# Sliding-window attention: computing the 64-query edge halves of the score blocks in sets of their own

## Chip, cores, metric

One Trainium2 chip, one core of it. The metric is the device time of one execution in microseconds (us), median of several. A profile is one execution; its span is some 2 us shorter than the time (339.9 against 341.89 us before). A quoted median is that of all executions. A ratio of two kernels is the mean time of the one's fast runs over that of the other's of the same rounds on the same chip, so it is not quite the ratio of the medians quoted beside it.

## What is computed

A transformer block on 2048 tokens of 640 features, bf16: adaptive layer norm, attention with 32 heads of 20 features in a causal window of 256 keys, residual, adaptive layer norm, gated MLP of width 1536, residual.

```python
mod = (_silu(c) @ w_mod).reshape(c.shape[0], 6, 1, -1)   # sa, ca, ga, sb, cb, gb
h = _layernorm(x, axis=-1) * (1 + ca) + sa
# attention: H = 32, Dh = 20, W = 256
mask = (idx[:, None] - idx[None, :] >= 0) & (idx[:, None] - idx[None, :] < W)
p = _softmax(jnp.where(mask[None, None], scores, -1000000000.0), axis=-1)
x = x + ga * attention(h)
h = _layernorm(x, axis=-1) * (1 + cb) + sb
x = x + gb * ((_sigmoid(h @ w_gate) * (h @ w_up)) @ w_down)
```

## The kernel before

A recording layer collects all operations with what they read and write. A list scheduler with a cost model, steered by tuned priorities (the table TIMES), then gives each engine its fixed order; at run time each engine takes its instructions in that order and waits on semaphores. Loads and stores all go through one issuing engine, in order as well.

The tokens are worked in six chunks of 2, 2, 4, 4, 2, 2 blocks of 128. For one group of four heads (they lie in four row groups of TensorE) a score set fills up to 512 columns for each head of one PSUM tile of four banks:

```python
def sc(e, eng, st=st, Sp=Sp):                     # scores, keys on partitions
    for (g, kb, q0, n) in st:                     # n blocks of 128 queries against key block kb
        for j in range(4):
            ins = mm(e, Sp.ap[:, j, off:off + n * 128],
                     kt.ap[32 * j:32 * j + DH, gl, (kb % 4) * 128:(kb % 4) * 128 + 128],
                     qt.ap[32 * j:32 * j + DH, gl, (q0 % 4) * 128:(q0 % 4 + n) * 128],
                     True, True, tp=(32 * j, 0))
        off += n * 128
# ... exponential S -> E on ScalarE (ACT), mask in place on GpSimd, then O += V'E on TensorE
p_S = Pool("S", [nc.alloc_psum_tensor("S0", [128, 4, 512], F32)])           # one buffer
p_E = Pool("E", [sb(f"E{i}", [128, 4, 512])[:] for i in range(4)] + ...)     # and weights not yet or no more in use
p_x1 = sbpool("x1", 8, [128, D]);  p_stg = sbpool("stg", 6, [128, 512]);  p_V = sbpool("V", 10, ...)
```

A key block of 128 meets three query blocks; in the first and in the last of them half of the products are masked away.

The softmax here doesn't subtract the row's maximum and nothing guards it: scores larger than these inputs give would overflow.

## Time and profile before

| | before |
|---|---|
| time | 343.07 us (341.72 to 344.42) |
| span of the profile | 339.9 us |
| TensorE busy / idle | 330.0 / 9.9 us |
| mean granted TensorE clock | 0.999 |
| TensorE matmuls | 3813 |

"Busy" counts the time in which an engine executes; it says nothing of how fast. The granted clock says that: in the records it is 1.0 or 0.5. The lines of this profile are shown in the prediction. In all views PE is TensorE, PEld its weight loads, DVE VectorE, ACT ScalarE, POOL GpSimd and SP the engine that issues the transfers.

### The profile page before, as it was taken

What the parts mean: (1) busy time and instruction counts of PE and PEld (TensorE: products, weight loads), DVE (VectorE), ACT (ScalarE), POOL (GpSimd) and SP (SyncE); (2) the same over time, 40 slices, a digit from 0 to 9 for tenths busy, and PEclk for the clock granted to TensorE, in tenths of its full rate; (3) what the DMA queues carried; (4) which work ended last, traced back from release to release, by engine and by line L of the source; (5) the groups of instructions that cost most, each with busy time, mean ns of one, the idle gap of its engine ahead of it and who ended that gap; (6) DMA issues with size and microseconds to landing.
All of it is one profiled execution on the core that took longest, in us unless ns stands there. A gap on an engine that the chain in (4) does not pass through costs nothing.

```text
span 339.9 us, 9584 instructions
## 1 busy us (share of the span) xinstructions
PE 330.0 (97%) x3813; PEld 201.2 (59%) x3813; DVE 227.6 (67%) x493; ACT 226.9 (67%) x229; POOL 178.4 (52%) x301
## 2 busy tenths in 40 slices
PE   7799989999999999998999999999999999999996
PEld 2577646655555656564765433466545446788884
DVE  4576599999776889646977446398746874554432
ACT  1377878888888888896887798956678851022230
POOL 5132564797666999555675566656656850010000
PEclk9999999999999999999999999999999999999999
DMA  6966689889987752472064101302740122112101
GB/s 211 353 202 181 191 235 257 288 270 209 231 282 253 224 194 41 151 226 60 2 180 115 48 31 65 111 3 40 162 123 12 49 22 72 44 35 41 39 3 39
DMA packets 50990, 44.99 MB, mean 132 GB/s; under 512 B 16513, under 2 KB 46850, under 8 KB 50946
## 3 DMA queue, kind: packets, MB, share of 16 engines
q1 hardware_dynamic: 50946, 44.38, 45.4%
q8 instruction: 30, 0.49, 0.6%
q14 instruction: 14, 0.11, 0.1%
HBM read 28.90 MB, written 12.19 MB: 121 GB/s over the span
## 4 chain that ended last, share of the span: by engine, by line
PE 92%; DMA 4%; SPq 1%; DVE 1%; ACT 1%; issue 0%; ACTq 0%; DVEq 0%
PE M L842 74%; PE S L843 8%; PE O L843 7%; PE M L843 3%; DMA big<-in_w_mod_dram 2%; DMA oT<-doc 1%; SPq L764 1%; DMA doc<-On 1%; ACT hT L984 0%; DVE x L937 0%; DVE V L1020 0%; DVE hT L1005 0%; ACT stg L1019 0%; DVE x L1316 0%; DVE big L1306 0%
## 5 line engine op out<-in xcount | busy, mean ns | idle before, releaser
L1188 ACT ACTIVATE E<-S 128x2048 bf16<-128x2048 f32 (+1 forms) x64 | 118.0, 1844 | 20.9 <-PE S L843 19.6
L842 PE MATMUL M<-h2T,wgu 128*128 128x256 bf16 (+1 forms) x720 | 114.6, 309 | 0.0
L842 PEld LDWEIGHTS M<-h2T,wgu 128*128 128x128 bf16 x720 | 67.2, 98 | 36.6 <-issue 5.5
L1199 POOL TENSOR_SCALAR_AFFINE_SELECT E<-E 128x512 bf16<-128x512 bf16 x89 | 59.9, 683 | 23.3 <-ACT E L1188 21.6
L1201 POOL TENSOR_SCALAR_AFFINE_SELECT E<-E 128x512 bf16<-128x512 bf16 x78 | 50.4, 655 | 31.8 <-ACT E L1188 27.5
L1306 DVE SCALAR_TENSOR_TENSOR big<-sig,M 128x256 bf16<-128x256 f32 (+1 forms) x72 | 36.4, 506 | 41.7 <-PE M L842 20.2
L1304 ACT ACTIVATE sig<-M 128x256 f32<-128x256 f32 (+1 forms) x72 | 32.4, 452 | 44.1 <-PE M L842 43.5
L842 PE MATMUL M<-wd,big 128*128 128x320 bf16 x384 | 56.5, 299 | 0.0
L842 PEld LDWEIGHTS M<-wd,big 128*128 128x128 bf16 x384 | 36.5, 98 | 16.0 <-issue 1.7
L843 PE MATMUL S<-QT,KT 20*128 20x256 bf16 (+2 forms) x832 | 36.2, 258 | 0.0
L926 DVE BATCH_NORM_STATS2 st<-x 128x6 f32<-128x320 bf16 x64 | 27.3, 477 | 7.2 <-DMA x<-in_A_x_dram 7.1
L1249 DVE STREAM_TRANSPOSE T<-O 128x512 f32<-128x512 f32 x32 | 22.6, 708 | 12.6 <-PE O L843 12.5
L843 PEld LDWEIGHTS S<-QT,KT 20*128 20x128 bf16 x832 | 12.3, 92 | 26.5 <-ACT E L1188 9.4
L1316 DVE TENSOR_TENSOR x<-M,x 128x320 bf16<-128x320 f32 x32 | 15.5, 484 | 18.3 <-PE M L842 17.8
L842 PE MATMUL M<-wv,hT 128*128 128x320 bf16 x160 | 27.4, 300 | 0.0
L842 PE MATMUL M<-wo,oT 128*128 128x320 bf16 x160 | 25.8, 300 | 1.5 <-DMA oT<-doc 1.4
L932 POOL TENSOR_SCALAR st<-st 128x2 f32<-128x2 f32 (+1 forms) x11 | 3.0, 274 | 40.4 <-DVE st L929 40.4
L842 PE MATMUL M<-hT,wk 128*128 128x512 bf16 (+1 forms) x100 | 23.1, 354 | 1.1 <-DVE V L1020 1.0
L1258 DVE STREAM_TRANSPOSE On<-Tn 128x512 bf16<-128x512 bf16 x32 | 22.5, 704 | 0.5
L842 PE MATMUL M<-hT,wq 128*128 128x512 bf16 (+1 forms) x100 | 22.7, 356 | 0.0
L843 PE MATMUL O<-E,V 128*32 128x256 bf16 (+2 forms) x568 | 21.1, 262 | 0.0
L1019 ACT ACTIVATE stg<-M 128x512 bf16<-128x512 f32 (+1 forms) x31 | 16.5, 534 | 6.6 <-PE M L842 6.2
(85 smaller groups left out, 386.3 us busy)
## 6 DMA issues: line engine op xcount, KB each, us to landing
x<-in_A_x_dram SPq DMA_DIRECT2D x32, 160.0 KB, 4.1
big<-in_w_mod_dram SPq DMA_DIRECT2D x15, 320.0 KB, 5.5
doc<-On SPq DMA_DIRECT2D x16, 256.0 KB, 2.2
KT<-dk SPq DMA_DIRECT2D x6, 512.0 KB, 5.1
QT<-dq SPq DMA_DIRECT2D x6, 512.0 KB, 4.7
out_dram<-x SPq DMA_DIRECT2D x16, 160.0 KB, 1.8
wgu<-in_B_w_gate_dram SPq DMA_DIRECT2D x5, 384.0 KB, 4.1
dq<-stg SPq DMA_DIRECT2D x15, 128.0 KB, 3.2
```

What stands on the lines that cost most here:

```text
L842: return e.matmul(o, l, r, start=st, stop=sp, skip_group_check=True)
L843: return e.matmul(o, l, r, start=st, stop=sp, tile_position=tp, skip_group_check=True)
L926: ins = e.bn_stats(v(bi * 12 + j * 6, 6), src[bi].ap[:, j * 320:(j + 1) * 320])
L1019: return e.activation(dst(), src(), ACT.Copy)
L1188: A("act", lambda e, eng, E=E, Sp=Sp, ncol=ncol: e.activation(E.ap[:, :, 0:ncol], Sp.ap[:, :, 0:ncol], ACT.Exp, scale=SM_SCALE), c_act(4 * ...
L1199: return e.affine_select(ap, ap, pattern=[[0, 4], [1, 128]], compare_op=ALU.is_ge, fill=0.0, base=0, channel_multiplier=-1)
L1201: return e.affine_select(ap, ap, pattern=[[0, 4], [-1, 128]], compare_op=ALU.is_ge, fill=0.0, base=-1, channel_multiplier=1)
L1249: A("dve", lambda e, g: e.transpose(T1.ap[:], O.ap[:]), 0.71, reads=[O.r()], writes=[T1.r()], prio=4, tag="tr1")
L1258: A("dve", lambda e, g: e.transpose(On.ap[:, half * 512:half * 512 + 512], Tn.ap[:]), 0.71, reads=[Tn.r()], writes=[On.r(half)], prio=7, t ...
L1304: A("act", lambda e, g, pg=pg, sg=sg: e.activation(sg.ap[:, 0:W], pg.ap[:, 0:W], ACT.Tanh, scale=0.5), c_act(W), reads=[pg.r()], writes=[s ...
L1306: A("dve", lambda e, g, pu=pu, sg=sg, ft=ft: e.scalar_tensor_tensor(out=hv(ft), in0=sg.ap[:, 0:W], scalar=1.0, in1=pu.ap[:, 0:W], op0=ALU. ...
L1316: A("dve", lambda e, g, ps=ps, bi=bi, half=half: e.tensor_tensor(x1[bi].ap[:, half * 320:half * 320 + 320], ps.ap[:, 0:320], x1[bi].ap[:, ...
```

## The change

The intent: a key block's first and last 64 queries have only half of their keys valid. The change computes these halves with tiles of 64 keys by 64 queries, two of them (from two key blocks) on one set of columns: partitions 0 to 63 from the one, 64 to 127 from the other. Eight pairs make a set C of 512 columns with an exponential of its own. The main pieces get a set each, and the masks write the edges from C beside them into an E tile of 768 columns. 92 score sets become 76, 60 main ones and 16 of edges.

```diff
-PVLAG = 2
-PVG = [3, 3, 2, 3, 3, 3]
+PVLAG = 1
+PVG = [2, 2, 1, 2, 2, 2]
-    p_x1 = sbpool("x1", 8, [128, D])
+    p_x1 = sbpool("x1", 6, [128, D])
-    p_stg = sbpool("stg", 6, [128, 512])
+    p_stg = sbpool("stg", 5, [128, 512])
-    p_V = sbpool("V", 10, [128, H * VW + 10])
-    p_E = Pool("E", [sb(f"E{i}", [128, 4, 512])[:] for i in range(4)] + ...
+    p_V = sbpool("V", 9, [128, H * VW + 10])
+    p_E = Pool("E", [sb(f"E{i}", [128, 4, 768])[:] for i in range(3)] + ...
+    p_C = sbpool("C", 1, [128, 4, 512])
...
+    def mmc(e, o, l, r, st, sp):                       # a full-array matmul as four of 32 columns of weights
+        for j in range(0, 128, 32):
+            ins = mm(e, o[j:j + 32], l[:, j:j + 32], r, st, sp, tp=(0, j))
...                                                     # early transposes of x:
-                            ins = mm(e, ps.ap[:, bi * 128:(bi + 1) * 128], ...
+                            ins = mmc(e, ps.ap[:, bi * 128:(bi + 1) * 128], ...
...
+                for (g, kb, hf, u, n, off) in items:    # hf: half of the key block, None for a main piece
+                    p0, kn = 64 * (hf or 0), 128 if hf is None else 64
+                    for j in range(4):
+                        ins = mm(e, Sp.ap[p0:p0 + kn, j, off:off + n * 64],
+                                 kt.ap[32 * j:32 * j + DH, gl, k0:k0 + kn],
+                                 qt.ap[32 * j:32 * j + DH, gl, q0:q0 + n * 64], True, True, tp=(32 * j, p0))
...
+                for (rule, c_, u) in spreads:           # edges: mask reads C, writes E
+                    mask(C, cu + c_, 1, E, u, rule, [C.r()])
...
-    (gate broadcast by 20 matmuls of 320 columns)
+    (gate as a column by 50 matmuls of 64 columns, transposed, written to memory and read back to all partitions)
-TIMES = { ... }
+TIMES = { ... }                                        # a new order for every engine
```

PVLAG and PVG say by how many sets the products with V follow the scores. Not shown here: the tables of priorities, the modulation sums in the S tile at the start, finer loads of the first weights, the last output in two halves. The early transposes are split because a split one keeps TensorE in the tiling of the projections around it (in the profile before a change of tiling costs about 0.11 us, worked out in the prediction).

## The prediction

What it reckons with, as the profile before shows it: full-array matmuls of 64, 256, 320 and 512 columns start 29, 109, 136 and 216 ns apart, thus 0.42 ns a column (2.4 GHz) and 2 to 3 ns a matmul. Its "cold matmuls" are those up to 4.7 us, where 512 columns take 0.43 us from start to start in place of 0.216. On GpSimd a memset of 64 columns takes 156 ns and one of 512 columns 525 ns.

> **What bounds the kernel now.** I read the page first: busy times, then the chain that ended last.
>
> ```profile
> span 339.9 us, 9584 instructions
> PE 330.0 (97%) x3813; PEld 201.2 (59%) x3813; DVE 227.6 (67%) x493; ACT 226.9 (67%) x229; POOL 178.4 (52%) x301
> ...
> PE 92%; DMA 4%; SPq 1%; DVE 1%; ACT 1%; issue 0%; ACTq 0%; DVEq 0%
> ```
>
> TensorE is on the chain for 92% of the span. Busy is not full speed, so I took the timeline of TensorE apart, from the start of one group of matmuls to the start of the next:
>
> ```profile
> 258.29 0.40 PE L843 MATMUL S<-QT,KT 20*128 20x128 bf16 x16
> 258.62 0.40 PE L843 MATMUL O<-E,V 128*32 128x256 bf16 x8
> ...
> 259.40 1.53 PE L842 MATMUL M<-wo,oT 128*128 128x320 bf16 x10
> 260.86 0.40 PE L843 MATMUL S<-QT,KT 20*128 20x256 bf16 x8
> ```
>
> A score set S streams 512 columns through four row tiles at once: 512 / 2.4 GHz = 0.213 us. It takes 0.33 us until the next group starts, so the change of tiling costs 0.117 us. The ten full-array matmuls should take 10 x (320 / 2.4 GHz + 3 ns) = 1.36 us and take 1.46: again 0.10. I use 0.11 us for each change of tiling. Over the whole instruction order, TensorE has 293.5 us of columns, 237 changes of tiling (26 us) and some 5 us of the 3 ns; the rest up to 339.9 is the start (first projection at 13.2 us, some 7 us of it lost), about 3 us of later idle gaps, the end (about 3 us) and cold matmuls.
>
> There is a second clock, the loop of the score sets. The next view is the timeline of TensorE and of ScalarE (ACT) in one stretch.
>
> ```profile
> 137.38 0.40 PE L843 MATMUL S<-QT,KT 20*128 20x384 bf16 x8
> ...
> 139.78 0.40 PE L843 MATMUL S<-QT,KT 20*128 20x256 bf16 x8
> ```
>
> ```profile
> 137.83 1.88 ACT L1188 ACTIVATE E<-S 128x2048 bf16<-128x2048 f32 x1 [0.52 <-PE S L843]
> 140.23 1.88 ACT L1188 ACTIVATE E<-S 128x2048 bf16<-128x2048 f32 x1 [0.52 <-PE S L843]
> ```
>
> There is one S tile of four PSUM banks, so a set must be read by its exponential before the next set is written: 0.40 (scores to their last end) + 0.05 + 1.88 + 0.07 = 2.40 us from start to start. That is the shortest spacing of two full sets. The kernel before runs at a median of 2.61 us, with other matmuls between, so this loop hardly costs TensorE anything today.
>
> [...] the trace has 40 of the 64-column modulation matmuls in 1.18 us, 29.5 ns each. [...] No run here shows yet how 64x64 score edges pack, which have eight tiles but only four row groups. [...]
>
> **The change part by part.** Each key block's first and last 64 queries have only half of the keys valid. The change computes these halves apart, with 64x64 tiles, eight edges to one set of 512 columns, and lets the mask write them into a 768-column E tile.
>
> 1. Score columns. Before, 84 sets of 512 and 8 of 384 columns = 46,080, or 19.2 us. After, 76 sets of 512 = 38,912, or 16.2 us. Saved 3.0 us. The gate's broadcast by 20 matmuls of 320 columns (2.7 us) becomes 50 of 64 columns (1.3 us) and a trip through memory. Saved in all **4.3 us**: the total of all columns goes from 293.5 to 289.1. PV keeps its 46,080 columns.
> 2. Changes of tiling. I counted them in the instruction order: 237 before, 211 after. 26 x 0.11 = **2.9 us** saved.
> 3. Start. The modulation sums move out of the M pool and are ordered so that only ten matmuls, not forty, follow the last landing (10.40 us, then 1.2 us of them). About **1 us** saved. The last output in two halves: **0.3 us**.
> 4. Small matmuls. TensorE gets 1114 more. 16 edge sets of 64 matmuls take 0.21 us if eight tiles run together, 0.43 if four[...]. I take **1.5 us** lost in all.
> 5. ScalarE. 92 exponentials become 76 and a few split ones: about 169 to 143 us. Off the path by itself; TensorE is the bound.
> 6. GpSimd. 240 masks of 512 elements before and after. At 0.68 us each (the L1199 group) a set's four masks take 2.7 us, which is as long as the loop, but 178 us of 340 leaves room, unless runs of 64 elements are slower.
>
> So far 4.3 + 2.9 + 1.3 - 1.5 = 7 us, a faster kernel by 2%.
>
> 7. The loop comes back. With less TensorE work between score sets, the instruction order after has places where two sets follow each other with less than 2.40 us of work between their starts. With the durations above, six early gaps and one that is a C set followed at once by a main set (2.07 us short) sum to 5.5 us short; the gaps in the last two-block chunk are 1.7, 1.1, 1.1, 1.9, 1.1 and 1.7 us, short by 5.7 us. TensorE takes its instructions in order, so it must wait: **11.2 us**, against 1.3 us by the same count before. Net **9.9 us** lost.
>
> Why is nothing else put there? The larger E tiles are paid for with SBUF: the pool x1 goes from 8 to 6 buffers. The output projection of the fourth chunk (four blocks) then gets its last two blocks only when the third chunk's down projection has released them. Before, it ended at 228.3 us and its normalisation ran beside that down projection:
>
> ```profile
> 228.29 0.49 DVE L1277 TENSOR_TENSOR x<-M,x 128x320 bf16<-128x320 f32 x1
> 228.70 1.66 DVE L926 BATCH_NORM_STATS2 st<-x 128x6 f32<-128x320 bf16 x4
> ...
> 242.41 1.69 DVE L948 TENSOR_SCALAR h2T<-h2T,scB,shB 128x512 bf16<-128x512 bf16 x5
> ```
>
> From the last residual add to the modulation are 14 us, which TensorE spent on other work. In the new order only 9.5 us of TensorE work lie between that last output projection and the chunk's first gate matmul. So some 5 us of waiting there follow from a second count too. These two counts describe the same idle time and are not added.
>
> Sum: 339.9 - 7.0 + 9.9 = 342.8 us of span. Some 3 us of idle before (waits for transfers) may fall into the same gaps, so I take 341. The profiled run was 2 us longer than its span (341.89 against 339.9); with the median at 343.07 and the fast run at 341.7, I write 342.5.
>
> **The rivals.** (a) TensorE's sum decides and the loop doesn't bite: 333 us of span, some 335 us. For it: 97% busy, and exponentials in the new kernel are fewer. Against it: the order is fixed, and the 2.40 us are measured. (b) The masks become the bound: with 64-element runs at 1 us a mask, four masks take 4 us a set, PV comes late and E buffers (five or six in place of seven, three in place of four in the third chunk) hold up exponentials: 350 us or more. The trace can't tell, since no such mask is in it; 683 ns for 512 elements is far from a fixed cost, so I expect no great change. (c) The gain is hidden behind transfers. The view of stretches (busy of PE, PEld, DVE, ACT, POOL; the last three columns are clock, DMA share, GB/s) has DMA 85% busy up to 100 us:
>
> ```profile
> 20.00:100.00 80.00, 78.83 (x1103) 48.51 (x1092) 64.71 (x144) 65.92 (x75) 48.91 (x75) 1.00 0.85 234
> 160.00:280.00 120.00, 119.98 (x1365) 63.26 (x1364) 82.61 (x173) 93.12 (x74) 76.30 (x120) 1.00 0.26 68
> ```
>
> The first gate matmul, at 106.2 us, can't run before its weights are there. Savings before it then vanish as idle time: 340 us of span. This pulls in the same direction as my step 7.
>
> **Range and chances.** Range 336 to 349: its low end is step 7 at a third of its size, its high end rival (b) in part. Faster by over 2% needs under 336.2 us, thus nearly no loop waits: 0.15. Slower by over 2%, over 349.9 us, needs masks or edges much dearer than taken: 0.08. Within 2%: 0.77.
>
> **What would show it.** Right: TensorE busy falls by several us while its idle time grows to some 15 to 20 us; matmuls of S wait for ACT E or ACT C; a hole of about 5 us between the last wo of the fourth chunk and its first wgu; first projection near 12.2 us; masks near 0.68 us; an edge set at 0.3 to 0.5 us. Wrong: masks at 0.9 us or more, TensorE idle time as before, or score sets nearer than 2.40 us.

## The result

| | before | after |
|---|---|---|
| time, us | 343.07 (341.72 to 344.42, 2 runs) | 365.86 (365.84 to 365.87, 2 runs) |
| ratio | | 1.0664, 95% interval 1.0484 to 1.0845: slower |
| span, us | 339.9 | 364.1 |
| TensorE busy / idle, us | 330.0 / 9.9 | 334.0 / 30.1 |
| mean granted clock | 0.999 | 0.977 |
| matmuls | 3813 | 4905 |

First the page of the kernel after: its size, the busy times, the clock in forty slices, and the chain of waits.

```profile
span 364.1 us, 11747 instructions
PE 334.0 (92%) x4905; PEld 213.5 (59%) x4927; DVE 229.1 (63%) x496; ACT 205.5 (56%) x221; POOL 182.7 (50%) x299
...
PEclk9969999989999989999999999999998999999999
...
PE 75%; POOL 7%; DMA 6%; DVE 5%; issue 4%; ACT 3%; SPq 0%; ACTq 0%; DVEq 0%; POOLq 0%
```

TensorE has gone from 92% of the chain to 75%. And there is something that the page before did not have: a third slice at 6, and single slices at 8. The view of stretches resolves them (busy of PE, PEld, DVE, ACT, POOL with counts; then clock, DMA share, GB/s), kernel after:

```profile
20.00:27.00 7.00, 5.19 (x79) 3.02 (x79) 3.64 (x10) 2.72 (x3) 2.54 (x4) 0.51 0.06 20
27.00:70.00 43.00, 40.92 (x805) 27.86 (x801) 28.83 (x68) 34.45 (x45) 21.62 (x33) 1.00 0.71 205
...
264.00:280.00 16.00, 10.26 (x262) 5.72 (x263) 12.94 (x26) 10.99 (x7) 12.00 (x19) 0.89 0.50 86
```

The clock records hold 0.5 for 6.83 us from 20.1, and for 3.41 us each from 71.3, 132.8 and 272.7. In these stretches full-array matmuls of 256 and 320 columns start 213 and 267 ns apart, against 109 and 136 elsewhere. TensorE was busy for 15.3 of these 17.1 us, so it did the work of 7.6 us: **7.6 us lost to the half clock**.

Second, the view of waits of TensorE: what it waited for, us in total, times, longest. Kernel before:

```profile
PE M L842 <- DMA big<-in_w_mod_dram: 2.0, 2, 1.0
PE M L842 <- DMA oT<-doc: 1.4, 1, 1.4
PE M L842 <- DVE V L1020: 1.4, 2, 1.0
...
```

Kernel after:

```profile
PE S L867 <- issue: 3.8, 2, 3.2
PE S L867 <- ACT C L1251: 3.3, 2, 2.0
PE M L866 <- issue: 3.2, 10, 1.7
PE M L866 <- DMA dq<-stg: 2.8, 2, 1.6
PE S L867 <- ACT E L1266: 2.2, 3, 1.2
...
PE O L867 <- POOL E L1236: 1.7, 2, 1.2
PE M L866 <- DMA x<-in_A_x_dram: 1.6, 2, 0.9
...
PE M L866 <- DVE h2T L985: 1.3, 2, 0.9
...
```

The whole list sums to 6.6 us before and 26.6 after. By kind, after less before: score sets waiting for an exponential 6.6; "issue" 7.0; the rest (transfers, masks, normalisation) 6.4. "Issue" means that the engine waited for nothing that the profile shows.

Part of this is no waiting. The trace after lacks the records of 22 matmuls of 512 columns (4905 matmuls, but 4927 weight loads; before, 3813 of each), the first of their groups. Where a gap stands in its place I fill in up to 0.216 us, the pace of such matmuls: 2.6 us in all, of which 1.5 are nine of the ten "issue" waits of M L866 (0.16 or 0.18 us each), 0.8 stand under other waits and 0.3 in gaps too short for the list. With this estimate the 24.2 us of span are

| | us |
|---|---|
| TensorE work at full clock: 334.0 + 2.6 - 7.6 against 330.0 | -1.0 |
| score sets waiting for exponentials | +6.6 |
| "issue" | +5.5 |
| other waits | +5.6 |
| half clock | +7.6 |
| gaps too short for the list | -0.1 |

Third, the "issue" waits. The longest lies inside the first edge set, in the timeline of TensorE (start, us, engine, line, operation, in brackets the idle time before):

```profile
17.93 0.52 PE L867 MATMUL S<-QT,KT 20*64 20x64 bf16 x41
21.61 0.39 PE L867 MATMUL S<-QT,KT 20*64 20x64 bf16 x23 [3.16 <-issue]
```

A wait between the 41st and 42nd matmul of one operation can have no semaphore. What moved at that time is in the list of DMA queues, first before, then after:

```profile
q8 instruction: 30, 0.49, 0.6%
```

```profile
q8 instruction: 39, 0.64, 0.7%
```

By its counts queue 8 brings TensorE's program: 39 packets of 16,384 bytes for 4927 weight loads and as many matmuls, so 253 of them a packet (252 to 256 in all 14 traces). One packet lies at 19.22 to 20.24 us, the one before it at 11.93. TensorE went on 1.37 us after the packet had landed. The traces of the changed kernel, of its variants and of b_split64 below have 15 "issue" waits of 0.4 us or more, and 14 of them end 1.2 to 1.6 us after such a packet has landed. I read that as TensorE standing with an empty program.

The halved clock at 20.1 us follows this gap, those at 71.3 and 132.8 follow gaps of 1.71 us ("issue") and 2.00 us (ACT C). This suggested theory A: **the many small matmuls outrun the supply of instructions and cost more than predicted, and every idle gap of some 2 us is charged twice, by the half clock that follows.** Rivals: C, the 64x64 matmuls are simply slow and nothing starves; D, the half clock has to do with the small matmuls and not with gaps; B, the new order waits for its late weights whatever TensorE does.

### The profile page after: what moved, and what is told of

It reads as the page before. It is cut to its first block, busy times and chain, and to the rows that moved or that the text cites.

```text
span 364.1 us, 11747 instructions
## 1 busy us (share of the span) xinstructions
PE 334.0 (92%) x4905; PEld 213.5 (59%) x4927; DVE 229.1 (63%) x496; ACT 205.5 (56%) x221; POOL 182.7 (50%) x299
## 4 chain that ended last, share of the span: by engine, by line
PE 75%; POOL 7%; DMA 6%; DVE 5%; issue 4%; ACT 3%; SPq 0%; ACTq 0%; DVEq 0%; POOLq 0%
PE M L866 58%; PE S L867 6%; PE O L867 5%; POOL E L1236 5%; PE M L867 3%; DMA x<-in_A_x_dram 2%; PE S L855 2%; ACT E L1266 1%; DMA big<-in_w_mod_dram 1%; DMA dk<-stg 1%; DMA dq<-stg 1%; DVE h2T L985 1%; POOL wd L1452 1%; POOL wq L1236 1%; DVE st L963 1%
## 5 line engine op out<-in xcount | busy, mean ns | idle before, releaser
L866 PE MATMUL M<-h2T,wgu 128*128 128x256 bf16 (+1 forms) x710 | 109.6, 309 | 2.1 <-DVE h2T L985 1.3
L1266 ACT ACTIVATE E<-S 128x2048 bf16<-128x2048 f32 (+2 forms) x46 | 81.1, 1765 | 18.9 <-PE S L867 18.3
L866 PEld LDWEIGHTS M<-h2T,wgu 128*128 128x128 bf16 x720 | 69.0, 98 | 36.0 <-issue 1.8
L1236 POOL TENSOR_SCALAR_AFFINE_SELECT E<-C 128x512 bf16<-128x512 bf16 x86 | 59.2, 709 | 29.5 <-ACT C L1251 25.6
L1236 POOL TENSOR_SCALAR_AFFINE_SELECT E<-E 128x512 bf16<-128x512 bf16 x86 | 57.6, 692 | 17.8 <-ACT E L1266 17.6
L866 PE MATMUL M<-wd,big 128*128 128x320 bf16 x384 | 55.7, 299 | 0.0
L867 PE MATMUL S<-QT,KT 20*64 20x64 bf16 (+3 forms) x1856 | 36.8, 216 | 10.4 <-issue 3.8
L866 PEld LDWEIGHTS M<-wd,big 128*128 128x128 bf16 x384 | 36.8, 98 | 15.4 <-DVE big L1380 0.3
L1251 ACT ACTIVATE C<-S 128x2048 bf16<-128x2048 f32 x16 | 30.0, 1877 | 20.9 <-PE S L867 20.7
L867 PEld LDWEIGHTS S<-QT,KT 20*64 20x64 bf16 (+1 forms) x1856 | 22.3, 100 | 32.1 <-issue 13.3
L866 PE MATMUL M<-wv,hT 128*128 128x320 bf16 x160 | 28.2, 315 | 2.8 <-issue 1.7
L866 PE MATMUL M<-wo,oT 128*128 128x320 bf16 x160 | 28.3, 310 | 1.7 <-DMA x<-in_A_x_dram 1.6
L866 PE MATMUL M<-hT,wk 128*128 128x512 bf16 (+1 forms) x92 | 21.0, 352 | 2.7 <-DMA dq<-stg 1.6
L867 PE MATMUL O<-E,V 128*32 128x128 bf16 (+2 forms) x584 | 21.6, 266 | 1.7 <-POOL E L1236 1.7
L866 PE MATMUL M<-hT,wq 128*128 128x512 bf16 (+1 forms) x96 | 21.7, 356 | 1.6 <-DMA dq<-stg 1.2
```

Source lines behind the costliest of these rows:

```text
L866: return e.matmul(o, l, r, start=st, stop=sp, skip_group_check=True)
L867: return e.matmul(o, l, r, start=st, stop=sp, tile_position=tp, skip_group_check=True)
L1236: return e.affine_select(units(E, du, 6), units(T, su, ss), pattern=[[0, 4], [0, 2], [rule[0], 64]], compare_op=ALU.is_ge, fill=0.0, base= ...
L1251: A("act", lambda e, eng, C=C, Sp=Sp: e.activation(C.ap[:], Sp.ap[:], ACT.Exp, scale=SM_SCALE), c_act(2048), reads=[Sp.r()], writes=[C.r() ...
L1266: return e.activation(E.ap[:].rearrange("p j (k c) -> p j k c", k=k)[:, :, :, 64 * u:64 * (u + n)], Sp.ap[:, :, off:off + 64 * n * k].rear ...
```

## The experiments

All were timed in three rounds (the last in five) beside the kernel before; its median on these chips was 343.3 to 344.3 us.

| run | of which kernel | time, us | ratio to before | TensorE idle, us | lost to the half clock, us |
|---|---|---|---|---|---|
| (the kernel after itself) | after | 365.86 | 1.0664 | 30.1 | 7.6 |
| a_e32 | after | 357.46 | 1.0393 | 28.2 | 7.7 |
| a_mm | after | 359.42 | 1.0450 | 24.0 | 8.2 |
| a_exphalf | after | 359.69 | 1.0484 | 26.3 | 5.0 |
| a_hold | after | 360.25 | 1.0474 | 25.7 | 7.4 |
| a_cdefer | after | 364.90 | 1.0600 | 27.9 | 8.7 |
| a_e32mm | after | 356.62 | 1.0365 | 26.0 | 6.1 |
| a_three | after | 354.59 | 1.0232 | 25.9 | 1.7 |
| b_split64 | before | 349.63 | 1.0150 | 17.8 | 1.5 |
| b_stall2, 3, 4 | before | 345.93, 349.38, 349.86 | 1.0042, 1.0144, 1.0170 | 16.8, 18.2, 18.6 | 1.7, 3.4, 3.4 |
| b_oT | before | 343.15 | 0.9966 | 13.4 | 0.0 |

The last two columns are of the profiled execution, worked out as above, and without the filling in: all of these traces lack some matmul records, so their idle times are somewhat too long.

### Edges as 32 matmuls instead of 64 (a_e32)

Each pair of 64x64 matmuls becomes one of 128 keys. This computes wrong edges (the comparison with the reference passed all the same, so it is no evidence here).

```diff
-                    items.append((g, kt_, 0, 2 * kt_, 1, off))
-                    items.append((g, kt_, 1, ...) if kb_ is None else (g, kb_, 1, 2 * kb_ + 5, 1, off))
+                    items.append((g, kt_, 2, 2 * kt_, 1, off))         # hf = 2: all 128 keys
```

> The changed kernel with its order of operations kept, but each score edge as one 128x64 matmul per head in place of two 64x64 ones: 32 instead of 64 matmuls per edge set, 1024 TensorE instructions (512 matmuls, 512 weight loads) fewer in all. The result is wrong on purpose. Theory A (the many small matmuls outrun the supply of instructions, TensorE stands still and its clock is then halved): the waits for 'issue' inside the edge sets (3.2 us at 18 us, 0.6 us at 42 us) and the halved clock at 20 to 27 us go, and an edge set falls from 0.5 to some 0.3 us: 9 to 13 us faster than the changed kernel, about 353. Theory B (the loop of score sets and the hole before the fourth chunk, as predicted): at most 3 us faster, 362 or more.

Measured: 357.46 us, 8.4 us less than the kernel after. An edge set and the start of the next group, after:

```profile
160.37 0.71 PE L867 MATMUL S<-QT,KT 20*64 20x64 bf16 x64
161.00 2.36 PE L866 MATMUL M<-h2T,wgu 128*128 128x256 bf16 x20
```

and in this run:

```profile
154.63 0.41 PE L867 MATMUL S<-QT,KT 20*128 20x64 bf16 x32
154.97 2.36 PE L866 MATMUL M<-h2T,wgu 128*128 128x256 bf16 x20
```

0.63 against 0.34 us from start to start: on average a 64x64 matmul takes 7.8 ns of TensorE and a 128x64 one 7.4. The average hides two paces. The edge set again, with the timeline cut after its 32nd matmul:

```profile
160.37 0.33 PE L867 MATMUL S<-QT,KT 20*64 20x64 bf16 x32
...
160.61 0.46 PE L867 MATMUL S<-QT,KT 20*64 20x64 bf16 x31
```

One of these matmuls lasts 0.21 us from start to end, so the first 32 started within 0.14 us: eight in 31 to 32 ns (3 to 4 ns from one to the next within each eight), where 128x64 tiles take 29 ns for four. Two halves of 64 keys do run beside each other. Then comes a pause of 99 ns, and from there on one matmul starts every 8.3 ns. The pause stands after the 32nd matmul in all 16 edge sets. After a longer stall inside a set the fast pace is back (in a_hold below the last 23 matmuls start within 0.10 us), so it is not the tiles that are slow, but the matmuls that come too slowly; why after 32 is not shown. 16 sets by 0.29 us are 4.6 us, an estimate; in the two profiles TensorE's busy time less the half clock fell by 3.8 us. The whole gain of 8.4 us is a little less than theory A wanted (9 to 13). The "issue" waits at 42 and 69 us are gone. But the early one is not: it moved by a few matmuls, into the transposes (2.82 us), and the half clock behind it stayed 6.83 us. Theory A had its place right and was wrong that this edit would end it.

### Early transposes unsplit (a_mm), and both (a_e32mm)

```diff
-                            ins = mmc(e, ps.ap[:, bi * 128:(bi + 1) * 128], ...
+                            ins = mm(e, ps.ap[:, bi * 128:(bi + 1) * 128], ...
```

> The changed kernel with its early transposes as one full-array matmul each in place of four of 32 rows (80 matmuls become 20; the instruction order and the result are the same). Theory A (TensorE outruns the supply of its instructions): 60 pairs of matmul and weight load fewer before the stall at 18.2 us, so TensorE gets some 120 instructions further before it starves; the stall of 3.16 us shrinks to about 2 us, and the halved clock behind it to one period of 3.4 us. Little of it reaches the end, since the first gate matmul waits for its weights: 363 to 365 us. Rival C (the 64x64 matmuls themselves are slow and nothing starves): stall as before, 365 to 366 us.

> Edges as 32 matmuls of 128x64 for a set, and the early transposes unsplit; same order, wrong result on purpose. Theory A: some 250 instructions fewer before 21 us, so the early stall (2.82 us with the first edit alone) falls below 1.5 us and no halved clock follows at 20 us: 354 to 356 us, 2 us or more under the first edit alone (357.5). Rival C: the same as the first edit alone, 357 us, with the stall in its place.

Measured for a_mm, which is correct: 359.42 us. 60 matmuls fewer, all in the first 24 us, take 6.4 us off the end. The 3.16 us "issue" wait became 0.91 us at 16.6, and no half clock followed at 20 us; "issue" waits in all fell from 5.5 to 0.9 us. The loss to the half clock did not fall, though (8.2 against 7.6 us): half clocks came at 104, 128, 261 and 272 us instead. The gain is idle time alone. I had expected too little (363 to 365): the last gate and up weights were issued at 119.9 us instead of 125.9, so the early gain passed through to them, against rival B. For a_e32mm: 356.62 us, just beyond the 354 to 356 expected, and only 0.8 us under a_e32, which is not clear of noise, where 2 us or more were expected; so beside a_e32 the early stall is worth little, and the two gains largely overlap. Its trace has 1.09 us of early wait and no half clock at 20 us. Rival C (nothing starves) is out.

### Moving the data away from the instructions (a_hold)

Every order stays; only the loads of the second chunk's activations and what follows them on the transfer queue wait until TensorE is just ahead of the first edge set.

```diff
+        held = [o for o in self.order["sp"] if o.grp == "x5@l1"][0]
+                        if o is held:
+                            engine.wait_ge(h(go.key), go.val)          # go: two operations before the first score set
```

> The changed kernel, every engine's order as it is; only the issue of the loads of the second chunk's activations and of what follows them on the transfer queue waits until TensorE is just ahead of the first edge set (about 17 us; before: issued from 13.2 us on). Theory A1 (the packets of instructions come late because they stand behind data in the transfer engines): with 640 KB fewer in front of it the packet of 19.2 us comes 1 to 2 us earlier and the stall of 3.16 us shrinks to under 2 us. Theory A2 (the supply has its own pace, one packet at a time, whatever data move): the packets come as before and the stall stays at 3 us. The time of the whole says little: the held loads come later themselves, 364 to 367 us; the stall in the trace decides.

Measured: 360.25 us, 5.6 us less than after, though loads were issued later; 364 to 367 had been expected. The DMA's busy tenths from 16 to 22 us in forty slices, after:

```profile
DMA  9999999999999999999999999954323201000000
```

and in a_hold, with its timeline at the same place:

```profile
DMA  9999997664610000000069389979778999999867
```

```profile
18.12 0.52 PE L873 MATMUL S<-QT,KT 20*64 20x64 bf16 x41
19.90 0.29 PE L873 MATMUL S<-QT,KT 20*64 20x64 bf16 x23 [1.27 <-issue]
```

With these data out of the way, the packet came at 17.52 instead of 19.22 us, TensorE stopped at the same 41st matmul, and the wait was 1.27 instead of 3.16 us; no half clock followed at 20 us. Here the packet had landed at 18.52 us, just before TensorE stopped, and TensorE went on 1.38 us after it, as in the kernel after (1.37). So in this run the packet of instructions came 1.70 us earlier without the data before it: it had stood behind them (A1), and the supply wasn't of a fixed pace (A2). As in a_mm, the half clock lost no less in all (7.4 us; it came at 128 and 264 us).

### The first edge set held back (a_cdefer)

```diff
+                            tmin=20.6 if edge and a == 0 and not last["s"] else 0.0,
```

> The changed kernel with its first edge set held back until the first value projections are done, so that it does not follow directly on 5 us of dense small matmuls while the transfers are backed up. Theory A: the 3.2 us wait in this set and the halved clock of 6.8 us after it go; against that, the order is about 3 us worse by the score loop's start: 3 to 6 us faster than the changed kernel. Theory B: 0 to 4 us slower.

Measured: 364.9 us; the three fast executions took 362.1 to 365.8, so no gain that is clear of noise, where theory A wanted 3 to 6 us. The early wait and the half clock at 20 us were gone, but here the scheduler made a new order, which its own cost model puts 3.0 us longer, and half clocks came at 71 (6.83 us), 119 (3.41 us) and 269 us (10.24 us). The run shows only that removing the early stall is not enough when the order changes with it; a_mm and a_hold, which keep the order, are the better test.

### The kernel before with small score matmuls (b_split64)

```diff
-                            ins = mm(e, Sp.ap[:, j, off:off + n * 128], ...
+                        for u in range(2 * n):                          # 64 columns each: 2112 matmuls more
+                                ins = mm(e, Sp.ap[:, j, off + 64 * u:off + 64 * u + 64], ...
```

> The kernel before, same order, with each score matmul cut into pieces of 64 columns: the same columns, 2112 matmuls and as many weight loads more. Theory A: waits for 'issue' of over 0.5 us appear, the clock may be halved somewhere, 5 to 25 us slower than before. Theory B says nothing of it: by columns alone no change, within 2 us[...].

Measured: 349.63 us, ratio 1.0150 (1.0073 to 1.0228). "Issue" waits appear in the kernel before too: three, of 0.46, 0.48 and 0.36 us, just short of the 0.5 expected (20 more of 0.16 or 0.18 us stand where the record of a matmul is missing). So small matmuls alone bring them, but twice the number that the change adds cost a quarter of its loss. So it must matter where they stand, and a_hold shows that busy transfers are part of it; no run varies the place alone.

### Shorter exponentials (a_exphalf)

From a buffer's second use, exponentials of full main sets and of edge sets cover two of four heads (wrong; 1.02 us each in place of 1.88), so the loop of score sets is some 1.5 us instead of 2.40.

```diff
+            jn = 2 if a or ob else 4                                   # likewise for E, once the buffer was full
-            A("act", ... e.activation(C.ap[:], Sp.ap[:], ...
+            A("act", ... e.activation(C.ap[:, 0:jn], Sp.ap[:, 0:jn], ...
```

> The changed kernel, same order on TensorE, but from the second use of a buffer on each exponential works on two of the four heads only (1.02 in place of 1.88 us; the result is wrong on purpose). It takes the loop of score sets away. Theory B: the waits of scores for exponentials (6.5 us of gaps) and two of the four stretches of halved clock (133 and 273 us) go: 8 to 12 us faster than the changed kernel. Theory A: 3 us or less.

Measured: 359.69 us, 6.2 us less than after, between what the two theories wanted. The waits of score sets for exponentials fell from 6.6 to 1.4 us, so the loop is their cause. Most of the gain is something else: in the profiles this run ends 6.5 us ahead, and 4.8 of them are there at 77 us already. 3.3 us come between 69 and 77 us, where the "issue" wait of 1.71 us and the half clock behind it did not occur. The edit changes no instruction of TensorE's, so why they did not is not shown. a_e32, a_mm and a_hold gain 2.3 to 2.8 us at the same place: each of these single gains contains this one event.

The loop's waits, as predicted from 2.40 us, are in the timeline of the kernel after near the end of the attention:

```profile
267.76 0.70 PE L867 MATMUL S<-QT,KT 20*64 20x64 bf16 x64 [1.16 <-ACT E L1266]
268.40 0.85 PE L866 MATMUL M<-wo,oT 128*128 128x320 bf16 x5
270.59 0.40 PE L867 MATMUL S<-QT,KT 20*128 20x192 bf16 x16 [1.33 <-ACT C L1251]
```

In this run that stretch waits for residuals and normalisation instead (DVE x 2.2 us, DVE h2T 1.9 us), and at 104 to 151 us it waits for masks (POOL E 4.1 us): part of the gain was taken by what came next in line. The early 3.19 us stayed.

### All three edits (a_three)

The edits of a_e32, a_mm and a_exphalf together.

> Both edits of the run before this one, and the exponentials of main sets on two of four heads (wrong result on purpose). If the three losses of theory A (supply of instructions, dearer edge sets, loop of the score sets) are separate, their gains add: 365.9 - 8.4 - 6.2 - 2 = 349 us. If they fill the same gaps and the loads of the gate weights set the pace: 353 to 356 us. What is left over the kernel before (343) is the new order with its smaller pools: about 6 us by the kernel's own scheduler.

Measured: 354.59 us. Two of the four executions were slow (357.2 both, granted clock 0.980 and 0.976); the fast ones took 351.6 and 352.0 at 0.995. So between the two expectations: the single gains (8.4, 6.4 and 6.2 us) do not add up to 21 us but to 14, as each contains the event at 70 us. In the profiled fast run TensorE is busy 324.4 us with at most 1.7 us of it lost to the clock; with 2.5 us for missing records that is 4.8 us less work than before, not far from what the prediction had hoped for, and yet TensorE is idle for 23.4 us, 13.5 us more than before, waiting for masks (4.3 us), loads of activations (1.9), normalisation and more. I put that part down to the new order and its smaller pools; this is argued, not shown. The kernel's own scheduler, which knows of neither the half clock nor the supply, puts the new order at 344.1 us against 338.5; no run divides this remainder further.

### An artificial gap in the kernel before (b_stall2, b_stall3, b_stall4)

In the dense tail, near 325 us, one gate matmul waits for memsets on GpSimd, two of 512, two of 1024, or all four.

```diff
+        stall = [o for o in self.order["pe"] if o.tag == "mlpg5"][8]
+                        if o is stall:
+                            engine.wait_ge(h("stall"), 1)
+                        engine.wait_ge(h(prev.key), prev.val)          # on GpSimd, after its last mask
+                        for t_ in self.scratch[:4]:
+                            ins = engine.memset(t_[:], 0.0)
+                        ins.then_inc(h("stall"), 1)
```

> The kernel before with one artificial wait of TensorE in the dense tail, near 321 us, for four memsets on GpSimd (about 3 us). Theory A (an idle gap of some 2 us or more brings a half clock for 3.4 us or a multiple): +3.1 us for the gap and 1.7 or 3.4 us for the halved clock, 4.8 to 6.5 us in all, about 348 us. Rival D (the halved clock in the changed kernel comes of something else, its small matmuls for instance): a gap of 3 us costs 3 us, 346 us, and the clock stays whole.

> The kernel before with an artificial wait of TensorE near 321 us as in the run with 2.98 us, but only about 1.0 us long. If there is a threshold between 1.4 us (a gap in the kernel before, after which the clock stayed whole) and 1.7 us (a gap in the changed kernel, after which it was halved): no halved clock, 33 + 80 matmuls at their usual pace, and the tail from the first of them to the end is 1.0 us longer than before (21.8 us). If any gap has its share of a halved clock: up to 2.7 us longer.

> The same with a wait of about 1.9 us. If the threshold lies between 1.4 and 1.7 us: a halved clock for 3.4 us, so the tail grows by 1.9 + 1.7 = 3.6 us. If only gaps longer than some 2 us do it: by 1.9 us.

The timeline with the short gap, then with the long one:

```profile
321.47 3.77 PE L852 MATMUL M<-h2T,wgu 128*128 128x256 bf16 x33
326.44 8.89 PE L852 MATMUL M<-h2T,wgu 128*128 128x256 bf16 x80 [1.20 <-POOL Tn L365]
```

```profile
321.84 3.77 PE L852 MATMUL M<-h2T,wgu 128*128 128x256 bf16 x33
328.59 10.56 PE L852 MATMUL M<-h2T,wgu 128*128 128x256 bf16 x80 [2.98 <-POOL On L365]
```

| gap, us | half clock, us | the 80 matmuls, us | from the 33 to the end, us | more than before (21.84) |
|---|---|---|---|---|
| 1.20 | none | 8.89 | 23.23 | 1.39 |
| 2.05 | 3.41 | 10.56 | 25.69 | 3.85 |
| 2.98 | 3.41 | 10.56 | 26.66 | 4.82 |

Full-array matmuls, nothing small near, and the same 80 take 1.67 us longer, half of 3.41, in both runs with a gap of over 2 us. Rival D is out.

The length of one gap is not what decides: gaps of 1.71, 1.75 and 1.93 us were followed by a half clock, one of 1.76 us was not, and one of 2.11 us in a_e32 (at 124.89) was not either. In all 14 traces the clock changes only at whole multiples of 3.41 us after its first record. So I cut each trace into these windows. The view of stretches for two windows in a row (first busy time: TensorE's; third number from the end: the clock), first around the 3.16 us of the kernel after, then around the 2.11 us of a_e32:

```profile
16.70:20.11 3.41, 1.75 (x93) 1.25 (x85) 0.74 (x2) 1.28 (x3) 0.00 (x0) 1.00 1.05 368
20.11:23.53 3.42, 1.72 (x46) 1.14 (x47) 1.14 (x3) 1.44 (x1) 0.00 (x0) 0.50 0.10 35
```

```profile
123.02:126.44 3.42, 1.87 (x45) 0.80 (x37) 1.71 (x3) 2.89 (x3) 1.28 (x2) 1.00 0.99 379
126.44:129.85 3.41, 2.18 (x49) 1.36 (x50) 1.89 (x3) 2.67 (x4) 2.84 (x5) 1.00 0.33 117
```

The first gap leaves 1.66 and 1.70 us idle in its two windows, and two windows of half clock follow; the second leaves 1.55 and 1.23 us, and none does. Over all 14 traces, up to the last matmul, TensorE at full clock was idle for 1.64 us or more in 23 windows, and the next window was at half clock after all 23; between 1.45 and 1.62 us after 4 of 14; below that after 2 of 1327. What counts here is thus the idle time summed within one window, about half of it, and two gaps of 1.33 and 0.93 us do it as well (the half clock at 272.7 us).

### A gap taken out of the kernel before (b_oT)

The kernel before has one such place: at 154 us TensorE waits for the attention output, 1.41 us in the profile shown, and 1.75 to 2.52 us in the profiles of b_split64 and of the three runs with a gap, a half clock following each time. Its scheduler is told that this transfer lands 2 us later, and puts other matmuls first.

```diff
+                if o.grp == "oT@a2":
+                    o.end += 2.0
```

> The kernel before with another place for the fourth projection's first matmuls: its scheduler is told that the attention output of the third chunk comes back from memory 2 us later, so it puts five chains of gate and up matmuls ahead of them. Before, TensorE waited there 1.41 to 2.5 us for that transfer, and in the executions with the longer waits the clock was halved once (granted clock 0.995 instead of 1.0, about 2 us longer). Theory A (an idle gap of over some 1.7 us costs itself and half of 3.4 us): with the gap gone, all executions stand at 1.0, the spread of 342 to 346 us shrinks, and the median falls by 1 to 2.5 us, to 341 to 342.5 us. Rival: the work moved forward is missing a little later, and the wait only moves: 343 to 344 us, with a gap elsewhere.

Measured: 343.15 us against 344.26 of the kernel before on this chip, ratio 0.9966 (0.9924 to 1.0008). The gap is 0.34 us. Three of the eleven executions of the kernel before were at a granted clock of 0.994 or 0.995 and took 345.0 to 346.0 us; all six of this one were at 1.0 (one of them, at 347.07 us, counts as slow by its time). That is what theory A expects. But one execution of the kernel before took 346.0 us at 1.0 as well, and the gain in time is not shown, since the interval holds 1.

## Why the prediction was wrong

It said 342.5 us, within 336 to 349; it was 365.86, slower. Step by step:

- **Work of TensorE (steps 1, 2 and 4: -4.3 - 2.9 + 1.5 = -5.7).** Measured -1.0, with the missing records filled in. The changes of tiling are as counted (237 and 211 in the traces). The mis-sized term is step 4, "I take **1.5 us** lost in all". It had the right question, whether eight tiles of 64x64 run together, and bet on a mixture of the two answers. They do, but for 32 matmuls only; with the pause and the slower pace after it an edge set takes 0.52 us (0.63 less a change of tiling), beyond even the 0.43 us thought of. 16 sets by 0.52 - 0.21 us are 5.0 us in place of 1.5, 3.5 of the 4.7 us that are missing; the other 1.2 are not traced. The clock it reckoned with, 2.4 GHz and 3 ns a matmul, fits: in the profile before, full-array matmuls of 256, 320 and 512 columns start 109, 136 and 216 ns apart.
- **Start (1 us).** The first projection came at 12.68 instead of 13.20 us: half of it.
- **The loop (step 7: 9.9 us).** The mechanism was right, the size too large: 6.6 us, 3.0 before 141 us and 3.5 near the end, the two places named. a_exphalf shows that the loop is their cause (1.4 us left). The hole of some 5 us before the fourth chunk's first gate matmul is right only in part: the stretch from 264 to 280 us has 5.7 us of idle time, but 3.5 of them are the loop's, and between the last wo and the first wgu there are 1.4.
- **ScalarE and masks (steps 5 and 6).** ACT fell from 226.9 to 205.5 us of busy time, and a mask takes 692 to 709 ns (0.68 foreseen). Rival (b), masks as the bound, did not happen, though masks are among the waits that the cheaper variants run into.
- **What the sum left out.** "Some 3 us of idle before (waits for transfers) may fall into the same gaps" and nothing else was the whole account of waiting outside the loop. Missing were the supply of instructions, 5.5 us of "issue" (a_mm and a_hold take most of it away), 5.6 us of other waits in the thinner order, and the half clock, 7.6 us. The prediction named "cold matmuls" once, for the kernel before (0.43 in place of 0.216 us each, up to 4.7 us), and gave the kernel after none; it counted an idle us as a us. Idle time of the loop's size did bring the clock down: gaps of 1.33 and 0.93 us in one window stand before the half clock at 272.7 us. This is the step that failed, the sum "339.9 - 7.0 + 9.9": of 5.7 us of work 1.0 was bought, and 17.6 us more of idle time and 7.6 us of slow clock were paid.

What stays open: the remaining 8 us or so of a_three over the kernel before, put down to the order and the pools together and not separated; and the loss to the half clock as a whole, which only a_exphalf, a_e32mm and a_three made smaller, none of them by an edit for it alone.

## What to carry to other kernels

Where TensorE is 97% busy, as it was here, ask what the next wait in line leaves of any work taken away from it: here 5.7 us were planned, 1.0 was bought, and 17.6 us of idle time came. Idle time cost a second time through the clock: after all 23 windows of 3.41 us with 1.64 us or more of it the next window was at half clock (1.67 us lost for a gap of 2.05 us). Count matmuls as well as columns: here splitting one into four cost 6.4 us where transfers were dense (a_mm: 60 matmuls in the first 24 us), and splitting one into halves 8.4 us (a_e32). The program itself came over the same transfer engines, in 39 packets of some 253 matmuls and weight loads each, and one packet came 1.70 us earlier when data were moved out of its way (a_hold). An "issue" wait in the middle of one operation that ends 1.2 to 1.6 us after a packet of the instruction queue has landed, as 14 of 15 did here, is the sign of that. And compare the counts of matmuls and weight loads first: where they differ (by 22 here), a short "issue" wait can be a missing record.
